# Attention over a cached K and V on one core: K transposed in 64-row tiles, P through the score banks, smaller loads

## The chip, the cores and the metric

One core of a Trainium2 chip. The metric is the device time of one execution in microseconds, lower is better; each time is the median of several executions. The kernel is one program with its own order of instructions for each of the five engines: TensorE (PE), VectorE (DVE), ScalarE (ACT), GpSimd (POOL) and SyncE (SP), which here issues the loads.

## The reference

Two independent blocks A and B, whose results are put side by side. For each of them:

```python
# x (16, 64, 640), k_cache and v_cache (16, 32, 512, 128), wq (640, 4096), wo (4096, 640), all bfloat16
q = (x @ wq).reshape(16, 64, 32, 128).transpose(0, 2, 1, 3)
scores = einsum("bhqd,bhkd->bhqk", q, k_cache) * 128 ** -0.5
p = softmax(scores, axis=-1)
o = einsum("bhqk,bhkd->bhqd", p, v_cache)
out = o.transpose(0, 2, 1, 3).reshape(16, 64, 4096) @ wo        # (16, 64, 640)
```

K and V of one batch and head are 512 x 128 values, 128 KB each. Over both blocks K and V are 268 MB, and every value is used once.

## The kernel before

**Tiling.** Two batches are worked on together, since 2 x 64 queries fill 128 partitions. A *step* g is one head of such a pair of batches, a *macro* m is two steps (two heads), a *chunk* c is four heads, a *group* is 16 heads of one pair of batches (`SPB` = 16 steps, four chunks). One pass holds half of the 32 heads of one block, so there are 4 passes of 8 groups, 32 groups, 128 chunks, 256 macros and 512 steps.

**One macro, operation by operation** (the names are those of the code; the line is that of the profile):
- LDK (L664) and LDV (L660) load K and V of four heads of one batch, 512 KB each, from SP's queue. LDWQ (L630) and LDWO (L638) load the weights of four heads, 640 KB each; LDX (L644) loads x by a transposing DMA.
- KX (L457): eight TensorE transposes, 128 rows by 128 columns, of K of both heads and one batch (index `sub`) into the bank KTB; each row of the K tile holds eight keys, so that the transposed order of the keys is permuted. KE (L466): VectorE copies the bank to `ktp_ring`.
- QP2 (L475): the queries of two heads, ten matmuls, into the first half of the bank QOB; QE2 (L484): ScalarE copies and scales them into `qT_ring`.
- SM (L496): scores of one step, one matmul for each batch in a 64-column tile of the array, into one of four score banks SB. MX (L505): negated row maximum on VectorE. EX (L511): exponential and row sum on ScalarE, into `p_ring`. RC2 (L517): reciprocals on VectorE. NM (L525): GpSimd scales P and puts its keys into the order of V, into `pn_ring`.
- TR2 (L534): eight transposes of P into the bank PTB. TE2 (L541, VectorE) or TA2 (L546, ScalarE, on 82 of the 256 macros) copies them to `pT_ring`.
- PV2 (L558): sixteen matmuls with V as the stationary operand, into the second half of QOB. OE2 (L566): ScalarE copies the result to `oT_ring`.
- OP2 (L574): two matmuls, the first 512 columns of the output, summed over the group in the bank OUTB. OX (L584): the last 128 columns, sixteen matmuls once per group, in score bank 0. OVP and OXP (L592, L597) store the sum of a first half of the heads, OVF and OXF (L602, L607) add that of the second half, and ST (L613) stores it to DRAM from ScalarE's queue.

**K by DMA.** In 11 of the 32 groups (`TGROUPS`) K of the second batch is not loaded plain and transposed on TensorE, but loaded by one transposing DMA for all 16 heads (LDKT, L651) into `kd_sb`; KX and KE with `sub` 1 are left out there.

**Order.** The order on PE, ACT, DVE and POOL is written out by hand for one chunk (two macros): a table for each engine with the kind, the offset in macros and a due time in a period of 6.7 us. The loads on SP are sorted by when they are needed and by when their buffer is free in that plan. The program then derives which instruction must wait for which from the buffers that they read and write, and drops the waits that others imply. Nothing is moved at run time: each engine runs its list in order and waits where it must. `NKB` = 4 chunks of K and `NVB` = 5 of V fit in SBUF, and `NW` = 6 weight slots of four heads.

The PSUM banks: 0 OUTB, 1 QOB, 2 to 5 SB, 6 PTB, 7 KTB.

Of the kernel before, what the change touches and what calls it, by code (L numbers as in the profile page):

```python
# [14 lines left out]
class Cfg:  # L15
    G = 4
    HH = 16
    NKB = 4
    NW = 6
    TGROUPS = (4, 6, 11, 13, 15, 19, 21, 23, 27, 29, 31)  # L20
    TLEAD = 1.0
    NVB = 5
    XLEAD = 1.5
    NQ = 3
    NKT = 5
    NP = 4
    NPN = 4
    NT = 2
    NO = 9
    NR = 8  # L30
    NS = 4
    PERIOD = 6.7
    PE_T = (("SM", 0, 0, 0.0), ("SM", 0, 1, 0.21), ("SM", 1, 0, 0.43), ("SM", 1, 1, 0.64), ("KX", 2, 1, 0.98),
            ("PV2", -3, 0, 1.43), ("TR2", -2, 0, 1.9), ("OP2", -4, 0, 2.35), ("KX", 3, 1, 2.78), ("QP2", 3, 0, 3.23),
            ("OP2", -3, 0, 3.79), ("OX", -3, 0, 4.2), ("KX", 3, 0, 4.22), ("PV2", -2, 0, 4.67), ("TR2", -1, 0, 5.14),
            ("KX", 4, 0, 5.59), ("QP2", 4, 0, 6.04))
    ACT_T = (("EX", 0, 0, 1.13), ("OE2", -3, 0, 2.1), ("EX", 0, 1, 2.49), ("TA2", -2, 0, 3.15), ("QE2", 3, 0, 4.0),
             ("EX", 1, 0, 4.4), ("OXP", -3, 0, 5.2), ("OE2", -2, 0, 5.34), ("EX", 1, 1, 5.73), ("OVP", -3, 0, 6.4),
             ("QE2", 4, 0, 6.65), ("ST", -3, 0, 6.68))
    DVE_T = (("MX", 0, 0, 0.44), ("MX", 0, 1, 1.06), ("RC2", -1, 0, 1.66), ("KE", 2, 1, 1.68), ("MX", 1, 0, 2.3),  # L40
             ("TE2", -2, 0, 2.6), ("RC2", 0, 0, 3.3), ("KE", 3, 1, 3.43), ("MX", 1, 1, 4.1), ("KE", 3, 0, 4.87),
             ("OXF", -3, 0, 5.3), ("OVF", -3, 0, 5.5), ("TE2", -1, 0, 5.79), ("KE", 4, 0, 6.4))
    POOL_T = (("NM", -1, 0, 1.95), ("NM", -1, 1, 2.8), ("NM", 0, 0, 4.2), ("NM", 0, 1, 5.05))
    TAIL_SPLIT = 2
    SLOT_NS = 3400.0
    DMA_NS = dict(LDK=3100.0, LDKT=9600.0, LDV=3100.0, LDWQ=3900.0, LDWO=4300.0, LDX=700.0)


class Op:
# [3 lines left out]
    def __init__(self, eng, kind, idx, reads=(), writes=(), dur=0.0, ts=None, aux=None):  # L53
        self.eng = eng
        self.kind = kind
        self.idx = idx
        self.reads = tuple(reads)
        self.writes = tuple(writes)
        self.sem = None
        self.count = None  # L60
        self.deps = []
        self.waits = []
        self.dur = dur
        self.ts = ts
        self.aux = aux
        self.dma = kind in ("LDK", "LDKT", "LDV", "LDX", "LDWQ", "LDWO", "ST")


def build_plan(dims, cfg):
# [3 lines left out]
    assert H % HH == 0 and HH % G == 0 and G % 2 == 0 and cfg.NR % 2 == 0 and B % 2 == 0  # L73
# [11 lines left out]
    MPP = NBP * MPG  # L85
    MPC = G // 2
# [11 lines left out]
    def by_dma(m, j=1):  # L98
        return j == 1 and m // MPG in cfg.TGROUPS

    tstart = [m for m in range(0, NMAC, MPG) if by_dma(m)]

# [3 lines left out]
    def kslot(m, j):  # L106
        return (4 * (m // 2) + (j if m % 2 == 0 else 3 - j)) % cfg.NKT

    def on_act(m):
        return m % 2 == 0 and not by_dma(min(m + 4, NMAC - 1))  # L110

    def make_op(kind, m, sub, ts):
        g0, g1 = 2 * m, 2 * m + 1
        if kind in ("KX", "KE") and by_dma(m, sub):
            return None
        ps_, bp, grp, h0 = step_info(g0)
        c = g0 // G
        if kind == "KX":
            return mk("pe", "KX", (m, sub), [("kn", c % cfg.NKB, g0 % G), ("kn", c % cfg.NKB, g1 % G), ("ident",)],
                      [("KTB",)], ts)  # L120
        if kind == "KE":
            return mk("dve", "KE", (m, sub), [], [("KTB",), ("ktp", kslot(m, sub))], ts)
        if kind in ("MX", "EX", "NM"):
            g = 2 * m + sub
            r = g % cfg.NR
            if kind == "MX":
                return mk("dve", "MX", g, [], [("SB", g % cfg.NS), ("negmax", r)], ts)
            if kind == "EX":
                return mk("act", "EX", g, [("negmax", r)], [("SB", g % cfg.NS), ("p", g % cfg.NP), ("rowsum", r)], ts)
            return mk("pool", "NM", g, [("p", g % cfg.NP), ("recip", r)], [("pn", g % cfg.NPN)], ts)  # L130
        r0, r1 = g0 % cfg.NR, g1 % cfg.NR
        if kind == "QP2":
            return mk("pe", "QP2", m, [("xT", bp), ("wq", wslot(ps_, h0 // G))], [("QOB",)], ts)
        if kind == "QE2":
            return mk("act", "QE2", m, [], [("QOB",), ("qT", m % cfg.NQ)], ts)
        if kind == "SM":
            kt = [("ktp", kslot(m, 0)), ("kd",) if by_dma(m) else ("ktp", kslot(m, 1))]
            return mk("pe", "SM", (m, sub), [("qT", m % cfg.NQ)] + kt, [("SB", (2 * m + sub) % cfg.NS)], ts)
        if kind == "RC2":
            return mk("dve", "RC2", m, [("rowsum", r0), ("rowsum", r1)], [("recip", r0), ("recip", r1)], ts)  # L140
        if kind == "TR2":
            return mk("pe", "TR2", m, [("pn", g0 % cfg.NPN), ("pn", g1 % cfg.NPN), ("ident",)], [("PTB",)], ts)
        if kind in ("TE2", "TA2"):
            if (kind == "TA2") != on_act(m):
                return None
            return mk("dve" if kind == "TE2" else "act", kind, m, [], [("PTB",), ("pT", m % cfg.NT)], ts)
        if kind == "PV2":
            return mk("pe", "PV2", m, [("pT", m % cfg.NT), ("v", c % cfg.NVB, g0 % G), ("v", c % cfg.NVB, g1 % G)],
                      [("QOB",)], ts)
        if kind == "OE2":  # L150
            return mk("act", "OE2", m, [], [("QOB",), ("oT", m % cfg.NO)], ts)
        if kind == "OP2":
            return mk("pe", "OP2", m, [("oT", m % cfg.NO), ("wo", wslot(ps_, h0 // G))], [("OUTB",)], ts)
        lo = grp * MPG
        last = h0 + 2 == SPB
        if kind == "OX":
            hi = m + 1
            if grp == NGRP - 1 and h0 + 6 == SPB:
                pass
            elif not last:  # L160
                return None
            elif grp == NGRP - 1:
                lo = m - 1
            return mk("pe", "OX", m, [("oT", i % cfg.NO) for i in range(lo, hi)]
                      + [("wo", wslot(ps_, i)) for i in sorted({(2 * i % SPB) // G for i in range(lo, hi)})],
                      [("SB", 0)], ts, aux=(lo, hi))
        if not last:
            return None
        if kind in ("OVP", "OXP") and ps_ % NHALF == 0:
            return mk("act", kind, m, [], [("OUTB",) if kind == "OVP" else ("SB", 0), ("outp", bp, kind[1])], ts,  # L170
                      aux=grp)
        if kind in ("OVF", "OXF") and ps_ % NHALF == 1:
            return mk("dve", kind, m, [("outp", bp, kind[1])],
                      [("OUTB",) if kind == "OVF" else ("SB", 0), ("out_sb", kind[1])], ts, aux=grp)
        if kind == "ST" and ps_ % NHALF == 1:
            return mk("act", "ST", m, [("out_sb", "V"), ("out_sb", "X")], [("out_dram", grp)], ts, aux=grp)
        return None

    templates = {"pe": cfg.PE_T, "dve": cfg.DVE_T, "pool": cfg.POOL_T, "act": cfg.ACT_T}
    at = {}  # L180
    for eng, tmpl in templates.items():
        offs = [t[1] for t in tmpl]
        for k in range(-(max(offs) + 1) // 2 - 1, (NMAC - min(offs)) // 2 + 1):
            for kind, off, sub, t in tmpl:
                m = 2 * k + off
                if 0 <= m < NMAC:
                    op = make_op(kind, m, sub, 2 * k + 2 * t / cfg.PERIOD)
                    if op is not None:
                        progs[eng].append(op)
                        at[kind, m, sub] = op.ts  # L190
# [10 lines left out]
    for ps_ in range(NPASS):  # L201
        for j in range(HG):
            m0 = ps_ * MPP + j * MPC
            i = ps_ * HG + j
            rq = ro = NEG
            if i >= cfg.NW:
                end = ((i - cfg.NW) // HG + 1) * MPP
                rq = at["QP2", end - MPG + ((i - cfg.NW) % HG) * MPC + MPC - 1, 0]
                ro = at["OX", end - 1, 0]
            add(rq, at["QP2", m0, 0], at["QP2", m0, 0], 0, "LDWQ", (ps_, j), [("wq", wslot(ps_, j))], (ps_, j),  # L210
                cfg.DMA_NS["LDWQ"] * G / 8.0)
            add(ro, at["OP2", m0, 0], at["OP2", m0, 0], 3, "LDWO", (ps_, j), [("wo", wslot(ps_, j))], (ps_, j),
                cfg.DMA_NS["LDWO"] * G / 8.0)

    def tload(m):
        return at["SM", m, 0] - cfg.TLEAD

# [540 lines left out]
```

## Time and profile before

| | us |
|---|---|
| median of 3 runs | 898.71 (897.31 to 901.26) |
| the profiled execution | 900.23 |
| its span, first to last instruction | 898.5 |
| PE busy | 857.5 |
| DVE, ACT, POOL busy | 746.6, 628.0, 413.8 |

The profile comes from one execution. Busy times sum the durations of an engine's instructions; since matmuls are pipelined and their ends are modelled, what a matmul costs is read from the distance of two starts. PEld is the loading of the stationary operand, which overlaps with PE. The granted TensorE clock was 0.996 of full speed in this execution. The loads move 292.06 MB on SP's queue.

### The profile page before, as it was taken

What the parts mean: (1) busy time and instruction counts of PE and PEld (TensorE: products, weight loads), DVE (VectorE), ACT (ScalarE), POOL (GpSimd) and SP (SyncE); (2) the same over time, 40 slices, a digit from 0 to 9 for tenths busy, and PEclk for the clock granted to TensorE, in tenths of its full rate; (3) what the DMA queues carried; (4) which work ended last, traced back from release to release, by engine and by line L of the source; (5) the groups of instructions that cost most, each with busy time, mean ns of one, the idle gap of its engine ahead of it and who ended that gap; (6) DMA issues with size and microseconds to landing.
All of it is one profiled execution on the core that took longest, in us unless ns stands there. A gap on an engine that the chain in (4) does not pass through costs nothing.

```text
span 898.5 us, 33204 instructions
## 1 busy us (share of the span) xinstructions
PE 857.5 (95%) x14016; PEld 691.1 (77%) x14144; DVE 746.6 (83%) x1398; ACT 628.0 (70%) x1651; POOL 413.8 (46%) x518
## 2 busy tenths in 40 slices
PE   4999989999999999999998998999999999999997
PEld 3777777878888877878786787778778777787875
DVE  2888878888888888888887887888888798888896
ACT  1776766777777777767676776777777676776774
POOL 0544444445444454544444444445454444545453
PEclk9999999999999999999999999999999999999999
DMA  9999999999999999999999999999999999999992
GB/s 304 336 340 365 318 272 365 295 361 365 363 366 368 286 361 322 319 369 270 364 361 368 367 260 365 309 324 366 294 363 363 367 370 284 367 286 365 315 333 77
DMA packets 315172, 296.81 MB, mean 330 GB/s; under 512 B 109200, under 2 KB 260752, under 8 KB 315024
## 3 DMA queue, kind: packets, MB, share of 16 engines
q1 hardware_dynamic: 312720, 292.06, 106.3%
q10 hardware_dynamic: 2304, 2.62, 0.9%
q8 instruction: 111, 1.82, 0.9%
q14 instruction: 37, 0.30, 0.1%
HBM read 266.34 MB, written 2.62 MB: 299 GB/s over the span
## 4 chain that ended last, share of the span: by engine, by line
PE 78%; DMA 9%; SPq 7%; DVE 3%; issue 1%; ACT 1%; DVEq 0%; ACTq 0%
PE ps L457 20%; PE ps L475 14%; PE ps L496 12%; PE ps L558 11%; PE ps L534 10%; PE ps L574 9%; DMA kn_ring<-in_B_k_cache_dram 5%; DMA kn_ring<-in_A_k_cache_dram 4%; SPq L651 3%; PE ps L584 3%; SPq L644 2%; DVE ktp_ring L466 1%; SPq L664 1%; DMA wq_sb<-in_A_wq_dram 1%; DVE negmax L505 1%
## 5 line engine op out<-in xcount | busy, mean ns | idle before, releaser
L525 POOL TENSOR_SCALAR pn_ring<-p_ring,recip 128x512 bf16<-128x512 bf16 x512 | 413.1, 843 | 476.1 <-DVE recip L517 475.7
L511 ACT ACTIVATE p_ring<-ps,negmax 128x512 bf16<-128x512 f32 x512 | 350.1, 684 | 100.0 <-DVE negmax L505 100.0
L466 DVE COPY ktp_ring<-ps 128x1024 bf16<-128x1024 bf16 x424 | 290.0, 684 | 82.1 <-PE ps L457 67.2
L505 DVE TENSOR_REDUCE negmax<-ps 128x1 f32<-128x512 f32 x512 | 337.3, 680 | 15.2 <-PE ps L496 4.9
L457 PEld LDWEIGHTS ps<-ident,kn_ring 128*128 128x128 bf16 x3392 | 205.3, 98 | 108.5 <-issue 46.5
L457 PE MATMUL ps<-ident,kn_ring 128*128 128x128 bf16 x3392 | 263.6, 221 | 21.1 <-DMA kn_ring<-in_A_k_cache_dram 11.8
L475 PE MATMUL ps<-xT_sb,wq_sb 128*128 128x128 bf16 x2560 | 187.8, 221 | 1.3 <-DMA wq_sb<-in_A_wq_dram 0.6
L558 PE MATMUL ps<-pT_ring,v_ring 128*128 128x64 bf16 x4096 | 162.0, 193 | 8.6 <-DMA v_ring<-in_B_v_cache_dram 3.1
L475 PEld LDWEIGHTS ps<-xT_sb,wq_sb 128*128 128x128 bf16 x2560 | 154.4, 99 | 16.9 <-ACT oT_ring L566 15.8
L558 PEld LDWEIGHTS ps<-pT_ring,v_ring 128*128 128x128 bf16 x4096 | 141.9, 98 | 28.5 <-issue 26.5
L484 ACT ACTIVATE qT_ring<-ps 128x256 bf16<-128x256 f32 x256 | 98.3, 384 | 86.1 <-PE ps L475 86.0
L534 PE MATMUL ps<-ident,pn_ring 128*128 128x128 bf16 x2048 | 156.4, 219 | 0.0
L566 ACT ACTIVATE oT_ring<-ps 128x256 bf16<-128x256 f32 x256 | 97.6, 381 | 75.3 <-PE ps L558 68.1
L541 DVE COPY pT_ring<-ps 128x1024 bf16<-128x1024 bf16 x174 | 119.5, 687 | 35.5 <-PE ps L534 35.5
L496 PE MATMUL ps<-ktp_ring,qT_ring 128*64 128x512 bf16 x848 | 137.3, 391 | 0.0
L574 PE MATMUL ps<-wo_sb,oT_ring 128*128 128x512 bf16 x384 | 124.5, 379 | 6.8
L534 PEld LDWEIGHTS ps<-ident,pn_ring 128*128 128x128 bf16 x2048 | 118.5, 98 | 0.0
L511 ACT ACTIVATION_READ_ACCUMULATOR p_ring<-ps,negmax 128x1 f32 x512 | 103.1, 201 | 0.0
L546 ACT ACTIVATE pT_ring<-ps 128x1024 bf16<-128x1024 bf16 x82 | 84.0, 1024 | 0.0
L496 PEld LDWEIGHTS ps<-ktp_ring,qT_ring 128*64 128x64 bf16 x848 | 47.1, 110 | 41.0 <-issue 2.1
L517 DVE RECIPROCAL recip<-rowsum 128x2 f32<-128x2 f32 x256 | 40.9, 160 | 14.7 <-ACT p_ring L511 14.6
L496 PE MATMUL ps<-kd_sb,qT_ring 128*64 128x512 bf16 x176 | 47.0, 390 | 0.0
(15 smaller groups left out, 152.0 us busy)
## 6 DMA issues: line engine op xcount, KB each, us to landing
v_ring<-in_A_v_cache_dram SPq DMA_DIRECT2D x128, 512.0 KB, 9.9
v_ring<-in_B_v_cache_dram SPq DMA_DIRECT2D x126, 512.0 KB, 9.8
kn_ring<-in_A_k_cache_dram SPq DMA_DIRECT2D x108, 512.0 KB, 9.4
kn_ring<-in_B_k_cache_dram SPq DMA_DIRECT2D x103, 512.0 KB, 9.3
wq_sb<-in_A_wq_dram SPq DMA_DIRECT2D x8, 640.0 KB, 9.9
wo_sb<-in_A_wo_dram SPq DMA_DIRECT2D x8, 640.0 KB, 10.7
wq_sb<-in_B_wq_dram SPq DMA_DIRECT2D x8, 640.0 KB, 9.7
wo_sb<-in_B_wo_dram SPq DMA_DIRECT2D x8, 640.0 KB, 10.3
```

The costliest lines, as they stand in the source:

```text
L457: ins = e.transpose(kt_ps[:, t8, :], kn_ring[:, c % NKB, j, hp, t8, :], ident[:, :])
L466: ins = e.tensor_copy(dst, src)
L475: ins = e.matmul(q_ps[:, sub * 128:(sub + 1) * 128], wq_sb[:, wslot(ps_, hh // G), kt, (hh % G) * DH:(hh % G + 1) * DH], xT_sb[:, kt, bp * ...
L484: ins = e.activation(qT_ring[:, m % NQ].rearrange("p s q -> p (s q)"), q_ps, ACTF.Copy, scale=scale)
L496: ins = e.matmul(s_bank(2 * m + sub)[64 * j:64 * j + 64, :], qT_ring[:, m % NQ, sub, 64 * j:64 * j + 64], kt, start=True, stop=True, tile_ ...
L505: ins = e.reduce_max(negmax[:, r:r + 1], s_bank(g), axis=AX.X, negate=True)
L511: ins = e.activation(p_ring[:, g % NP, :], s_bank(g), ACTF.Exp, bias=negmax[:, r:r + 1], scale=1.0, accum_out=rowsum[:, r:r + 1])
L525: ins = e.tensor_scalar(dst, src, recip[:, r:r + 1], 1.0, ALU.mult, ALU.mult)
L534: ins = e.transpose(pt_ps[:, sub, t, :], pn_ring[:, g % NPN, t * 128:(t + 1) * 128], ident[:, :])
L541: ins = e.tensor_copy(pT_ring[:, m % NT].rearrange("p s t q -> p (s t q)"), pt_ps_flat)
L558: ins = e.matmul(o_ps[:, col:col + 64], v_ring[:, c % NVB, j, gi, t, :], pT_ring[:, m % NT, sub, t, 64 * j:64 * j + 64], start=(t == 0), s ...
L574: ins = e.matmul(out_ps, oT_ring[:, m % NO, sub, :], wo_sb[:, wslot(ps_, hh // G), hh % G, 0:N0], start=(hh == 0), stop=(hh == SPB - 1))
```

## The change

- K: KX takes both batches of a macro at once. `kn_ring` becomes ten units of one macro; each unit has two tiles (one per batch) with the rows of head 0 in partitions 0 to 63 and of head 1 in 64 to 127. A transpose takes 64 rows (one head) instead of 128; the two heads alternate between the upper and the lower half of the array's rows (`tile_position`) and write to two banks (6 and 7). 32 transposes of 64 rows replace 2 x 8 of 128. KE copies both banks with one copy of 2048 elements per partition.
- P: TR writes a full tile (both steps of a macro) into score bank 0 or 1, in turn, instead of a bank of its own. TE copies it, on VectorE for even macros and on ScalarE for odd ones. `pT_ring` has four slots, not two.
- QP4, QE4, PV4, OE4 work on four heads at once where QP2, QE2, PV2, OE2 worked on two, and share the whole bank QOB. OX moves to score bank 2, always sixteen matmuls.
- No LDKT: all of K is transposed on TensorE, and `kd_sb` is gone.
- Loads: LDK and LDV are 256 KB each (two heads of one batch), LDWQ and LDWO are cut in two. Each load on SP waits until the fifth load before it has landed (`NDMA` = 5).
- The order written out for each engine is new, for a period of 6.15 us.

The core of the diff:

```diff
-    NKB = 4
+    NKU = 10
-    TGROUPS = (4, 6, 11, 13, 15, 19, 21, 23, 27, 29, 31)
-    NQ = 3
-    NKT = 5
+    NQ = 4
+    NKT = 3
-    NT = 2
-    NO = 9
+    NT = 4
+    NO = 10
-    PERIOD = 6.7
...
+    PERIOD = 6.15
+    PE_T = (("SM", 0, 0, 0.0), ("SM", 0, 1, 0.21), ("SM", 1, 0, 0.43), ("SM", 1, 1, 0.64), ("KX", 2, 0, 0.96),
+            ("PV4", -2, 0, 1.53), ("OP", -5, 0, 2.47), ("TR", -2, 0, 2.9), ("KX", 3, 0, 3.45), ("TR", -1, 0, 4.03),
+            ("OP", -4, 0, 4.47), ("OX", -5, 0, 4.9), ("QP4", 2, 0, 4.92))
+    ACT_T = (("EX", 0, 0, 1.13), ("EX", 0, 1, 1.79), ("OVP", -5, 0, 2.92), ("OE4", -2, 0, 2.95), ("EX", 1, 0, 3.52), ("EX", 1, 1, 4.18),
+             ("TE", -1, 0, 4.84), ("OXP", -5, 0, 5.9), ("ST", -5, 0, 6.0), ("QE4", 2, 0, 6.27))
+    DVE_T = (("MX", 0, 0, 0.44), ("MX", 0, 1, 1.06), ("KE", 2, 0, 1.68), ("RC2", 0, 0, 2.83), ("OVF", -5, 0, 2.92),
+             ("MX", 1, 0, 2.97), ("MX", 1, 1, 3.59), ("TE", -2, 0, 4.21), ("KE", 3, 0, 4.83),
+             ("OXF", -5, 0, 5.9), ("RC2", 1, 0, 5.98))
+    NDMA = 5
...
+    for op, old in zip(progs["sp"][cfg.NDMA:], progs["sp"]):
+        op.deps.append(old)
...
-        OUT_BANK, QO_BANK, PT_BANK, KT_BANK = 0, 1, 6, 7
+        OUT_BANK, QO_BANK, S_BANK0, KT_BANK = 0, 1, 2, 6
+        kt_ps = [ps[:, KT_BANK + r, :].bitcast(BF16) for r in range(2)]
+        kt_ps_both = ps[:, KT_BANK:KT_BANK + 2, :].bitcast(BF16)
+        ox_ps = ps[:, S_BANK0 + 2, 0:N1]
+        def pt_bank(m):
+            return ps[:, S_BANK0 + m % 2, :].bitcast(BF16)
...
         def em_KX(e, op):
-            for t8 in range(8):
-                ins = e.transpose(kt_ps[:, t8, :], kn_ring[:, c % NKB, j, hp, t8, :], ident[:, :])
+            for j in range(2):
+                for t in range(8):
+                    for r in range(2):
+                        half = slice(64 * r, 64 * r + 64)
+                        ins = e.transpose(kt_ps[r][:, 64 * (8 * j + t):64 * (8 * j + t) + 64],
+                                          kn_ring[half, op.idx % NKU, j, t, :], ident[half, half],
+                                          tile_position=(64 * r, 0))
...
         def em_KE(e, op):
+            ins = e.tensor_copy(ktp_ring[:, op.idx % NKT].rearrange("d r j s -> d r (j s)"), kt_ps_both)
...
+        def em_TR(e, op):
+                    ins = e.transpose(pt_bank(m)[:, 128 * i:128 * i + 128],
+                                      pn_ring[:, (2 * m + sub) % NPN, t * 128:(t + 1) * 128], ident[:, :])
...
+        def em_LDK(e, op):
+            src = blocks[blk][1][2 * bp + j, h0:h0 + 2].rearrange("hs (p t) d -> (hs p) (t d)", t=8)
+            ins = e.dma_start(kn_ring[:, m % NKU, j].rearrange("p t d -> p (t d)"), src)
...
+        def em_LDV(e, op):
+            src = blocks[blk][2][2 * bp + j, h0:h0 + 2].rearrange("g (p t) d -> p g (t d)", p=128)
+            ins = e.dma_start(v_ring[:, c % NVB, j, n:n + 2].rearrange("p g t d -> p g (t d)"), src)
```

## The prediction

> **What bounds the kernel now.** I read the page first, then the time line of TensorE over one steady period, then the windows view for the load side, then the waits.
>
> ```profile
> span 898.5 us, 33204 instructions
> PE 857.5 (95%) x14016; PEld 691.1 (77%) x14144; DVE 746.6 (83%) x1398; ACT 628.0 (70%) x1651; POOL 413.8 (46%) x518
> ...
> GB/s 304 336 340 365 318 272 365 295 361 365 363 366 368 286 361 322 319 369 270 364 361 368 367 260 365 309 324 366 294 363 363 367 370 284 367 286 365 315 333 77
> ```
>
> TensorE is busy 95% of the span, so its work per chunk is the first price. The second line to see is GB/s: it stands at 360 to 370 except in slices that hold a DMA transpose of K. One normal chunk on TensorE, from one score group (L496) to the next:
>
> ```profile
> 227.99 1.05 PE L496 MATMUL ps<-ktp_ring,qT_ring 128*64 128x512 bf16 x8
> 228.98 0.62 PE L457 MATMUL ps<-ident,kn_ring 128*128 128x128 bf16 x8
> 229.43 0.63 PE L558 MATMUL ps<-pT_ring,v_ring 128*128 128x64 bf16 x16
> 229.90 0.61 PE L534 MATMUL ps<-ident,pn_ring 128*128 128x128 bf16 x8
> 230.56 0.38 PE L574 MATMUL ps<-wo_sb,oT_ring 128*128 128x512 bf16 x1
> 230.78 0.61 PE L457 MATMUL ps<-ident,kn_ring 128*128 128x128 bf16 x8
> 231.23 0.72 PE L475 MATMUL ps<-xT_sb,wq_sb 128*128 128x128 bf16 x10
> ...
> 234.72 1.05 PE L496 MATMUL ps<-ktp_ring,qT_ring 128*64 128x512 bf16 x8
> ```
>
> Start to start is what counts, not the duration: 8 transposes of K take 0.45 us (56 ns each), 16 PV matmuls of 64 columns 0.47 (29.3 ns each), 10 query matmuls 0.65 into the scores but 0.55 elsewhere. The period is 6.73 us; where batch 1 of K comes by DMA it is 5.85 (two transposes of 8 fewer), and the output rest (L584) adds 0.89 once in four chunks. TensorE has no holes in it.
>
> ```profile
> core 0: us, PE busy (x) PEld busy (x) DVE busy (x) ACT busy (x) POOL busy (x), PEclk, DMA share, GB/s
> 200.00:290.00 90.00, 89.31 (x1491) 73.36 (x1503) 78.19 (x145) 68.53 (x176) 42.18 (x52) 1.00 1.08 366
> 162.00:178.00 16.00, 15.89 (x272) 13.06 (x271) 13.60 (x26) 11.84 (x31) 6.70 (x9) 1.00 1.21 277
> ...
> SPq L664 <- PE ps L457: 75.0, 79, 3.5
> ```
>
> In 90 undisturbed us PE is busy 89.3 us and the DMA engines are full at 366 GB/s; with a K transpose in flight they are fuller still and move 277. SP waits for a K slot only 75 us in all. So there are two bounds close together: TensorE, and loads. All loads are 292.06 MB (queue q1), which is 798 us at 366.
>
> **TensorE after, per chunk.** A chunk becomes: scores 4 x 0.216 + 0.025 (the first pair's extra) = 0.889; PV 32 x 0.0293 = 0.938; out projection 4 x 0.216 = 0.864; P transposes 16 x 0.056 = 0.896; query 20 x 0.056 = 1.12. These are unchanged in number, only grouped by four heads. K transposes: 2 x 32 instructions of 64 rows and 64 columns, alternating between two row halves. No row shows a row tile. The nearest rows are two: PV gives 29.3 ns for one instruction of 64 columns with its own weights, and the scores (L496), which use two column halves, show that two halves run side by side: 8 matmuls of 512 columns take 0.99 us, where one at a time would be 8 x 0.216 = 1.73; in the trace the second of a pair starts 4 ns after the first. So a pair costs 29.3 ns if the halves overlap and 58.6 if not. I take the first, because the pair of L496 is the nearer row: same engine, tiles, alternating halves. A group is then 16 x 0.0293 + 0.025 = 0.494, two per chunk 0.988, against 4 x 0.45 = 1.79 now.
>
> Changing the tile shape costs too: from the query to the scores the gap is 0.149 instead of 0.056, and from the last score to the next group 0.311 instead of 0.216, so 0.094 for each change. Now there are 2 per chunk. After it are 5 (query to scores, scores to K, K to PV, P to K, K to P): 0.47. The sum is 6.17. The same sum for the two periods of now gives 6.69 and 5.79 against 6.73 and 5.85, so I add 0.05: **6.22 us** per chunk. Bounds of a change: 0 to 0.15 (the whole gap). Bound of the added waits (each K group waits for two loads, each PV for four): the gap before a K group with two waits after P is 0.092 rather than 0.056, that before a PV with two waits is 0.056, so 0 to 0.036 each for about 8, up to 0.29 per chunk or 37 us; I take none, since most stand at a tile change, which drains anyway.
>
> **The other engines.** VectorE start to start is 0.60 for a row maximum, 0.60 for a copy of 1024, 0.07 to 0.24 for a reciprocal. After: 4 maxima, 1 copy of P, 2 reciprocals and 2 copies of 2048. No row shows 2048; between 0.60 (as 1024) and 1.20 (twice), I take 1.13 (0.60 plus the 0.53 that 1024 elements stream). Sum 2.4 + 0.6 + 0.4 + 2.3 = 5.7, at worst 5.9: hidden by TensorE's 6.22, with little left. The group's last additions (0.59 and 0.20) fall where TensorE has 0.89 more. ScalarE: 4 x 0.66 + 0.94 + two copies of 512 at most 2 x 0.56 = 4.7. GpSimd 4 x 0.81 = 3.2. P transposes into banks 0 and 1 wait for this chunk's exponentials of those banks, and the next scores wait for the copies out; by the order written, the first exponential ends some 1.8 us after the scores start and the first P group starts at 2.9 (0.89 + 0.09 + 0.49 + 0.09 + 0.94 + 0.43), and the copies out end before the next scores by 0.5 to 1.4. Both waits are covered; what covers them is that slack.
>
> **Loads.** Bytes stay; the transposes by DMA go (11, each 17.9 us to landing, with the engines at 268 to 304 GB/s around them). New is the cap: load n waits until load n-5 landed, everything behind it on SP waits too, and TensorE waits for that. Five loads hold 1.31 MB, 3.58 us at 366. What a load needs empty: 1.2 us from issue to the first packet (first K load), 0.5 from the last packet to the landing (last V load), 0.72 of data, 2.4 in all, below 3.58. The lone 160 KB store landed in 1.8. SP issues a load in 0.34 to 0.56 us when nothing backs up; 8.5 per chunk are 4.3. So the cap should not starve the engines: rate 366; the lowest undisturbed rows are 349 and 350 (V alone, below), and a starved queue would give less (rival 2). TensorE asks for 2.28 MB per 6.44 us on average, 354 GB/s. The price is that both bounds nearly meet.
>
> At this place a rule speaks against the change. The Trainium skill, "DMA: Bandwidth & Descriptors", section "Rules for kernel authors", asks for at least 1 MiB per DMA. The trace does not bear that out under a queue: the last four V loads are 256 KB and 872 to 876 and 875 to 880 us moved 349 and 350 GB/s, V alone, as 512 KB loads of V did.
>
> **Sum.** First scores at about 14 us (18.9 now; less is loaded ahead of them: 2.5 MB, at 366 that is 6.9 after the first packet at 3.4, then a query group and the scores); 127 periods x 6.22 = 790; 31 x 0.89 = 28; from the last scores to the end 15 (14.9 now; the chain through exponential, transposes, PV, output and store stays). Together 847, plus 4 for loads at the pass boundaries, where now some 20 us go. Span 851, with 1.7 around it 853; the median of the runs lies 1.5 below the profiled execution now (898.71 against 900.23), so **851**. The load bound alone gives 3 + 798 + about 6 after the last V = 807. Half a per cent, 4.5 us, is about what the runs can tell from no change.
>
> **Rivals.**
> 1. Row halves do not overlap (slower). Then 32 slots of 29.3 ns: 0.47 more per group, 256 groups, 120 us: **971**. For it: no row shows a row tile, every transpose loads 128 columns of weights, and PV never goes below 28 ns. Against: L496. It decides from (898.7 - 851) / 256 = 0.19 us more per group, 41 ns per pair. 0.13. The Trainium skill, "TensorE: Matmul & The Clock Gate", section "Wait — 56ns, not 53.3ns?", says that starts never come closer than about 25 ns however few the columns; by that rule a group is 0.80 and the time about 851 + 0.33 x 256 = 935. The trace disagrees for column halves (4 ns), and shows nothing for row halves.
> 2. The five-load cap starves the engines. At rate r the time is 292/r + 9: 866 at 341, 898 at 328. Any rate under about 347 sets the end. Each 0.05 us of gap per load costs 1094 x 0.05 = 55 us, less the 44 by which the load bound lies below. Between 866 and 894: 0.10; slower than 903: 0.07.
> 3. A chain of waits sets the period, not TensorE: the score banks now serve P too, and VectorE has half a us left. 0.2 to 0.3 more per chunk is 876 to 890. 0.10.
> 4. The edits cancel (the gain of the transposes is paid as tile changes of 0.15 and waits): 894 to 903, 0.04.
>
> **How the numbers follow.** My case, 838 to 866, has 0.52; below 838 (fewer drains, K to PV free) 0.04. Faster is 0.52 + 0.04 + 0.10 + 0.10 = 0.76, same 0.04, slower 0.13 + 0.07 = 0.20. The range runs from 836 to 900: above it lie the 0.20 of the slower cases, so 0.8 is inside.
>
> **What would show it.** Right: score groups 6.2 us apart, K groups (32 instructions) 0.5 to 0.6 from first start to the next group's, pairs a few ns apart; GB/s flat at 350 to 366. Rival 1: K groups of 0.8 to 1.0. Rival 2: PE idle before L457 or L558 on DMA, SP's queue waiting for landings, GB/s flat below 345. Rival 3: TensorE waiting for VectorE or ScalarE before scores or P. The forecast is wrong if the span lies outside 836 to 900, and its reason is wrong if K groups take over 0.7 or the period over 6.5.

## The result, and the profile after

The changed kernel takes **1020.74 us** (median of 4 runs, 1018.52 to 1029.17) against 899.99 us (897.31 to 901.37) for the kernel before on the same chip: a ratio of 1.136, 95% interval 1.132 to 1.140. The forecast was 851, with a range of 836 to 900. The profiled execution took 1020.85 us, its span was 1019.1. Here and below, ratios and intervals compare executions in the faster of two states of the chip, while medians are over all executions.

The page of the changed kernel, parts 1 to 4 and 6:

```profile
span 1019.1 us, 44106 instructions
PE 856.1 (84%) x18944; PEld 656.4 (64%) x18944; DVE 730.7 (72%) x1184; ACT 651.1 (64%) x1441; POOL 416.3 (41%) x518
...
GB/s 261 307 305 284 284 296 305 273 287 299 282 308 305 290 297 299 302 295 288 271 306 313 317 295 285 292 299 295 278 286 288 309 290 290 309 296 301 297 315 179
...
q1 hardware_dynamic: 242880, 292.10, 89.5%
...
DMA 89%; SPq 4%; PE 4%; issue 1%; DVE 1%; ACT 0%; DVEq 0%; ACTq 0%
...
kn_ring<-in_A_k_cache_dram SPq DMA_DIRECT2D x256, 256.0 KB, 4.5
```

No engine is the bound: TensorE went from 95% to 84% busy. The load rate is flat at 261 to 317 GB/s up to the last slice, where before it stood at 360 to 370 in the slices without a transposing load of K. Part 4 names the cause: 89% of the chain that ended last is waiting for a transfer. (The granted TensorE clock was 0.975 in this execution and 0.996 before; with TensorE on 4% of that chain, it is not what costs the 121 us.) And a load of 256 KB takes 4.5 us from issue to landing. TensorE in two chunks, from its time line:

```profile
405.00 1.05 PE L441 MATMUL ps<-ktp_ring,qT_ring 128*64 128x512 bf16 x8
405.99 0.64 PE L409 MATMUL ps<-ident,kn_ring 64*128 64x64 bf16 x32
407.35 1.09 PE L500 MATMUL ps<-pT_ring,v_ring 128*128 128x64 bf16 x32 [0.72 <-DMA v_ring<-in_A_v_cache_dram]
...
413.31 1.05 PE L441 MATMUL ps<-ktp_ring,qT_ring 128*64 128x512 bf16 x8
414.30 0.64 PE L409 MATMUL ps<-ident,kn_ring 64*128 64x64 bf16 x32
414.87 1.11 PE L500 MATMUL ps<-pT_ring,v_ring 128*128 128x64 bf16 x32
415.81 0.60 PE L516 MATMUL ps<-wo_sb,oT_ring 128*128 128x512 bf16 x2
416.24 0.61 PE L479 MATMUL ps<-ident,pn_ring 128*128 128x128 bf16 x8
416.79 0.64 PE L409 MATMUL ps<-ident,kn_ring 64*128 64x64 bf16 x32
417.36 0.62 PE L479 MATMUL ps<-ident,pn_ring 128*128 128x128 bf16 x8
417.81 0.59 PE L516 MATMUL ps<-wo_sb,oT_ring 128*128 128x512 bf16 x2
418.25 1.28 PE L425 MATMUL ps<-xT_sb,wq_sb 128*128 128x128 bf16 x20
419.46 0.84 PE L441 MATMUL ps<-ktp_ring,qT_ring 128*64 128x512 bf16 x6
```

The chunk from 413.31 to 419.46 is undisturbed, 6.15 us, and each K group (L409, 32 instructions) is 0.57 us from its start to the next group's. That is the TensorE that was forecast. The first chunk shows what became of it: PV (L500) stands 0.72 us for a V load. The waits of TensorE and of SP's queue, two views:

```profile
PE ps L500 <- DMA v_ring<-in_A_v_cache_dram: 61.8, 50, 2.5
PE ps L500 <- DMA v_ring<-in_B_v_cache_dram: 50.0, 43, 2.4
```

```profile
SPq L604 <- DMA kn_ring<-in_B_k_cache_dram: 67.1, 163, 2.5
SPq L595 <- DMA v_ring<-in_B_v_cache_dram: 58.3, 106, 2.6
SPq L604 <- DMA kn_ring<-in_A_k_cache_dram: 57.8, 157, 1.6
SPq L595 <- DMA v_ring<-in_A_v_cache_dram: 56.5, 108, 3.6
```

Each line is: who waited, for what, us in total, times, longest. SP stands before its K loads (L595) and V loads (L604) until an earlier load has landed, 240 us by these four rows alone; before, its longest row was 75 us for a free K slot. The queue is throttled by the cap, not by space. The middle of the run in the windows view (length, PE, PEld, DVE, ACT, POOL, then granted clock, DMA share, GB/s):

```profile
300.00:500.00 200.00, 172.09 (x3871) 132.26 (x3872) 150.26 (x246) 130.11 (x286) 84.44 (x104) 0.98 0.92 293
```

The semaphore records of this window show more of the 4.5 us. The end of a load is told by 16 signals, as many as there are DMA engines. The first comes 2.70 us after the issue, and the last, which is the landing, 1.6 us after the first (medians). The next load goes only when the last signal of the oldest one is there, so five loads move 5 x 0.262 MB / 4.5 us = 291 GB/s, against 293 measured.

### The profile page after: what moved, and what is told of

Same layout as the page of the kernel before. It is cut to its first block, busy times and chain, and to the rows that moved or that the text cites. A ratio compares the mean times of both kernels' runs of the same rounds, so it can differ in the third digit from the quotient of the medians.

```text
span 1019.1 us, 44106 instructions
## 1 busy us (share of the span) xinstructions
PE 856.1 (84%) x18944; PEld 656.4 (64%) x18944; DVE 730.7 (72%) x1184; ACT 651.1 (64%) x1441; POOL 416.3 (41%) x518
## 3 DMA queue, kind: packets, MB, share of 16 engines
q8 instruction: 151, 2.47, 1.0%
q10 hardware_dynamic: 2304, 2.62, 0.7%
HBM read 289.41 MB, written 2.62 MB: 287 GB/s over the span
## 4 chain that ended last, share of the span: by engine, by line
DMA 89%; SPq 4%; PE 4%; issue 1%; DVE 1%; ACT 0%; DVEq 0%; ACTq 0%
DMA v_ring<-in_A_v_cache_dram 24%; DMA kn_ring<-in_B_k_cache_dram 22%; DMA kn_ring<-in_A_k_cache_dram 21%; DMA v_ring<-in_B_v_cache_dram 20%; SPq L587 2%; SPq L595 2%; DMA wq_sb<-in_B_wq_dram 2%; PE ps L500 1%; DMA wq_sb<-in_A_wq_dram 1%; PE ps L516 1%; SPq L604 1%; PE ps L479 1%; PE ps L409 1%; DMA wo_sb<-in_A_wo_dram 0%; PE ps L425 0%
## 5 line engine op out<-in xcount | busy, mean ns | idle before, releaser
L417 DVE COPY ktp_ring<-ps 128x2048 bf16<-128x2048 bf16 x256 | 312.7, 1222 | 29.3 <-PE ps L409 28.9
L500 PE MATMUL ps<-pT_ring,v_ring 128*128 128x64 bf16 x4096 | 145.0, 195 | 114.8 <-DMA v_ring<-in_A_v_cache_dram 61.8
L500 PEld LDWEIGHTS ps<-pT_ring,v_ring 128*128 128x128 bf16 x4096 | 132.2, 99 | 127.1 <-issue 125.3
L409 PEld LDWEIGHTS ps<-ident,kn_ring 64*128 64x128 bf16 x8192 | 138.7, 96 | 92.1 <-issue 73.5
L409 PE MATMUL ps<-ident,kn_ring 64*128 64x64 bf16 x8192 | 168.4, 193 | 23.0 <-DMA kn_ring<-in_B_k_cache_dram 12.9
L425 PE MATMUL ps<-xT_sb,wq_sb 128*128 128x128 bf16 x2560 | 167.4, 222 | 14.5 <-DMA wq_sb<-in_A_wq_dram 12.3
L516 PE MATMUL ps<-wo_sb,oT_ring 128*128 128x512 bf16 x512 | 158.2, 392 | 5.2 <-DMA wo_sb<-in_A_wo_dram 3.6
L488 ACT ACTIVATE pT_ring<-ps 128x1024 bf16<-128x1024 bf16 x128 | 131.1, 1024 | 31.0 <-PE ps L479 28.2
L490 DVE COPY pT_ring<-ps 128x1024 bf16<-128x1024 bf16 x128 | 88.0, 688 | 80.9 <-PE ps L479 80.2
L508 ACT ACTIVATE oT_ring<-ps 128x512 bf16<-128x512 f32 x128 | 76.3, 596 | 106.8 <-PE ps L500 105.7
L434 ACT ACTIVATE qT_ring<-ps 128x512 bf16<-128x512 f32 x128 | 76.4, 597 | 89.4 <-PE ps L425 89.4
L516 PEld LDWEIGHTS ps<-wo_sb,oT_ring 128*128 128x128 bf16 x512 | 36.7, 100 | 6.9 <-DMA wo_sb<-in_A_wo_dram 4.2
```

What stands on the lines that cost most here:

```text
L409: ins = e.transpose(kt_ps[r][:, 64 * (8 * j + t):64 * (8 * j + t) + 64], kn_ring[half, op.idx % NKU, j, t, :], ident[half, half], tile_pos ...
L417: ins = e.tensor_copy(ktp_ring[:, op.idx % NKT].rearrange("d r j s -> d r (j s)"), kt_ps_both)
L425: ins = e.matmul(qo_ps[:, i * 128:(i + 1) * 128], wq_sb[:, wslot(ps_, hh // G), kt, i * DH:(i + 1) * DH], xT_sb[:, kt, bp * 128:(bp + 1) * ...
L488: ins = e.activation(dst, pt_bank(op.idx), ACTF.Copy)
L490: ins = e.tensor_copy(dst, pt_bank(op.idx))
L500: ins = e.matmul(qo_ps[:, col:col + 64], v_ring[:, c % NVB, j, i, t, :], pT_ring[:, (2 * c + i // 2) % NT, i % 2, t, 64 * j:64 * j + 64], ...
```

## The experiments

The first theory, **C**: the cap of five starves the DMA engines, whatever the size of a load. Its first rival, **S**: loads of 256 KB are slow however many are under way. The quoted expectations name theories by these letters and say what others hold where they bring them in. Times below are medians, with the ratio to the kernel before and its 95% interval. A *stop* is a place where two neighbouring matmuls of one group start more than 350 ns apart, after the first 30 us; its us are this distance of the starts.

**Without the cap, and with a cap of eight.**

```diff
-    NDMA = 5
+    NDMA = 100000
```

> The changed kernel without the cap: no load waits for the landing of another, only for its buffer. Theory C (the cap): five loads of 256 KB are too few, because a load takes 4.5 us from issue to landing in the changed kernel and not the 2.4 to 3.6 of the sum; without the cap the rate goes from 292 to 350 to 366 GB/s, TensorE no longer waits for loads, the score groups stand 6.15 us apart (as they do in the changed kernel wherever no load is late), and the time is 840 to 865 us. Theory S (the size): loads of 256 KB are slow by themselves; then the rate stays near 290 to 300 GB/s and the time within 2% of 1020. Theory M (the memory side: the changed kernel's own work slows the transfers): as S.

```diff
-    NDMA = 5
+    NDMA = 8
```

> The changed kernel with eight loads under way instead of five (2.1 MB instead of 1.3). Theory C: the rate rises with the bytes under way and nears the full 366 GB/s; landing takes 5.7 to 6.2 us, the time is 850 to 890. Theory S and M: within 2% of 1020, only the landing takes longer (about 7 us).

Without the cap: 947.53 us (1.053, 1.049 to 1.057). With eight: 900.37 us (1.003, 0.9998 to 1.006). So the cap is the larger part of the loss (taking it away gives back 73 us, raising it to eight 120, of 121 against the kernel before), and S falls, and with it M, by which the changed kernel's own work slows the transfers: loads of 256 KB move 360 GB/s and more once eight are under way. But both runs miss the range that C gave, neither comes near 851, and the uncapped one is slower than the one capped at eight, which C does not explain. The rate with the cap of eight, then rate and chain of the uncapped kernel:

```profile
GB/s 279 366 344 361 328 368 358 365 363 363 366 240 366 367 365 368 369 335 305 366 297 240 360 331 332 360 358 367 362 362 270 350 370 369 366 370 346 324 146 16
```

```profile
GB/s 289 363 343 368 326 366 319 326 319 347 332 139 368 369 369 320 316 326 314 364 269 224 368 304 356 367 287 332 353 363 159 341 369 369 318 337 329 327 162 15
...
PE 82%; issue 8%; SPq 4%; DVE 3%; ACT 1%; DMA 1%; POOL 0%; DVEq 0%; ACTq 0%
```

Waiting for transfers is down from 89% of the chain to 1%. New is 8% of "issue", time in which an engine waits for nothing that the profile shows. On TensorE's time line of the same kernel it looks like this:

```profile
143.32 0.55 PE L409 MATMUL ps<-ident,kn_ring 64*128 64x64 bf16 x25
145.81 0.29 PE L409 MATMUL ps<-ident,kn_ring 64*128 64x64 bf16 x7 [1.94 <-issue]
```

A group of 32 stops after its 25th instruction, where there is no wait in the program, for 2.1 us from start to start. There are 81 such stops, 87 us in all, and 65 of them (80 us) end 1.0 to 1.8 us, in the median 1.41 us, after a packet of 16 KB of the instruction queue (q8) has ended; 13% of the run's time lies at such a distance from a packet, so chance would give some 10. From this came theory **I**: with a deep load queue, TensorE's next instructions arrive late. Its first rival, **W**, holds that the rest of the loss is waiting among the engines. The page of the kernel after counts 151 packets of 16 KB, the page before 111; an instruction and its weight load are two, so a chunk has 296 instructions after and 221 before, and 256 of them, one packet (2.47 MB over 37,888 instructions are 65 bytes each), last 5.3 us at a period of 6.15 where they lasted 7.8 at 6.73.

**Loads of 512 KB with the cap of five.**

```diff
-                add(ready, first, first, 2, "LDK", (m, b), [("kn", m % cfg.NKU, b)], (m, b), cfg.DMA_NS["LDK"])
+            add(ready, first, first, 2, "LDK", (m, 0), [("kn", m % cfg.NKU, b) for b in range(2)], (m, 0), 2 * cfg.DMA_NS["LDK"])
...
-                add(ready, first, first, 2.5, "LDV", (c, i), [("v", c % cfg.NVB, i)], (c, i), cfg.DMA_NS["LDV"])
+                add(ready, first, first, 2.5, "LDV", (c, j), [("v", c % cfg.NVB, i) for i in (2 * j, 2 * j + 1)], (c, j), 2 * cfg.DMA_NS["LDV"])
...
```

> The changed kernel with K and V loads of 512 KB (both batches of a macro for K, four heads of a batch for V), still at most five under way. Theory C, bytes under way count: 2.6 MB, 350 to 366 GB/s, 840 to 870 us. Theory S: the loads are as large as before the change, so it is the same number; it differs from C only beside the run without the cap. Theory M: near 1020.

933.47 us (1.040, 1.034 to 1.045), far above the 840 to 870 that C gave. Five loads now hold 2.62 MB. Waits for loads are 6% of the chain, so the starving is gone, but there are 77 stops of 74 us. A cap in loads acts as a cap in bytes: in stops and time, five of 512 KB (2.4 MB under way in the median) lie between eight of 256 KB (2.1) and no cap (2.5).

**The cap alone, in the kernel before.** Three loads of 512 KB are 1.57 MB, a little more than the 1.31 of the change. Each load of K and V got a counter of its own for this.

```diff
...
+    for op, old in zip(progs["sp"][3:], progs["sp"]):
+        op.deps.append(old)
```

> The kernel before with one thing added: a load waits until the third load before it has landed, so that 1.5 MB are under way instead of 3.3 (6 to 7 loads). Each of its K and V loads gets its own semaphore for this. Theory C: the kernel before is slowed as well, to 300 to 325 GB/s between the DMA transposes, 980 to 1060 us. Theory S and M: it stays within 2% of 899, since sizes and work are the same.

1032.2 us (1.151, 1.144 to 1.158): as slow as the change, with nothing else of it. The windows view, of a stretch without transposing loads of K and of one with three of them:

```profile
200.00:290.00 90.00, 82.21 (x1316) 65.70 (x1317) 67.77 (x126) 59.58 (x156) 37.03 (x46) 0.96 0.94 307
300.00:500.00 200.00, 176.38 (x2801) 140.23 (x2799) 149.07 (x282) 120.81 (x321) 81.90 (x102) 0.95 0.99 292
```

Without a cap this kernel moved 366 GB/s in its stretch of 200 to 290 us and 335 in 300 to 500; with the cap it moves 307 and 292. Theory C holds from both sides, and S and M, by which this kernel should have stayed at 899, fall.

**Caps of seven and six.**

```diff
-    NDMA = 5
+    NDMA = 7
```

> The changed kernel with seven loads under way. The first four runs left two costs that go opposite ways: with five the loads are starved (292 GB/s, TensorE waits for K and V), without the cap TensorE stops in the middle of runs of equal matmuls, 81 times for 87 us in all, each time ending 1.3 to 1.5 us after a 16 KB packet of the instruction queue; with eight 43 times for 36 us. Theory I: many bytes of loads under way delay the fetch of TensorE's instructions. Then seven has fewer such stops (15 to 35 us) and loads at 340 to 350 GB/s when wanted, 885 to 930 us. Theory W (the rest with eight is waiting among engines, the cap does nothing to it): seven is slower than eight by the loads alone, 910 to 950, with as many stops as eight.

```diff
-    NDMA = 5
+    NDMA = 6
```

> The changed kernel with six loads under way (1.6 MB). Theory I and the cap: hardly any stops in mid-run (under 15 us), loads at 310 to 330 GB/s, 920 to 970 us. Theory W: the same time or above, but with some 36 us of stops in mid-run, as with eight.

Seven: 891.85 us (0.990, 0.986 to 0.993), the first version faster than the kernel before, by 1%. Six: 938.55 (1.042, 1.037 to 1.047). Bytes under way over the landing time give the rate: 6 x 0.262 / 4.85 = 324 GB/s (323 measured in 300 to 500 us), 7 x 0.262 / 5.2 = 353 (344 measured). From five to seven, one more under way lengthens a load by only 0.35 us. Bytes are not the whole of it: six loads of 256 KB moved 323 GB/s, the three of 512 KB in the kernel before, as many bytes, 307. The chain with seven:

```profile
DMA 58%; PE 34%; SPq 4%; issue 2%; DVE 1%; ACT 1%; DVEq 0%; ACTq 0%
```

Both losses are smaller here, but both are there: waiting for loads, and 19 stops of 13 us (15 to 35 us of them were expected). With six the stops are 7 of 4 us, where W asked for some 36 us.

**Is it the row halves that stop?** K by full tiles of 128 rows, 16 transposes per macro instead of 32, without a cap. Everything else of the change stays, but that the copy KE now puts the keys in order.

```diff
-    NDMA = 5
+    NDMA = 100000
...
-                    for r in range(2):
...
+                    ins = e.transpose(kt_ps[j][:, 128 * t:128 * t + 128], kn_ring[:, op.idx % NKU, j, t, :], ident[:, :])
...
```

> The changed kernel without the cap, and with K transposed in full 128-row tiles again: 16 transposes per macro instead of 32, so TensorE has 29,700 instructions with the weight loads instead of 37,900, and its period is longer, 6.15 + 2 x (0.896 - 0.494) - 3 x 0.094 = 6.67 us. Theory I: the stops in mid-run all but vanish, as in the kernel before (8 of them, 4 us), although as many loads are under way as in the run without the cap; the score groups are 6.6 to 6.7 us apart, 885 to 910 us, faster than the 947 without the cap in spite of the longer period. Theory W: the stops stay (60 us or more), 960 to 1000 us.

917.7 us (1.021, 1.019 to 1.023), a little above the range expected, with a period of 6.68 us and 3 stops instead of 81. Its loads are as deep in the queue as those of the uncapped change (2.9 MB under way in the median against 2.5, landing 7.9 to 8.2 us), so depth alone makes no stops. Its TensorE is hardly ever idle:

```profile
PE 889.1 (97%) x14720; PEld 735.5 (80%) x14848; DVE 727.8 (79%) x1184; ACT 650.8 (71%) x1441; POOL 417.8 (46%) x518
```

That leaves two readings: fewer instructions, or no row halves. The next run tells them apart.

**More instructions in the kernel before**, and no row halves: its query matmuls in two halves of 64 columns, its score matmuls in two of 256. The work is the same, the matmuls are 17,728 instead of 14,144.

```diff
+                for half in range(2):
+                    for kt in range(KT):
...
+                        ins = e.matmul(q_ps[:, c0:c0 + 64],
...
+            for half in range(2):
+                for j in range(2):
...
+                                   qT_ring[:, m % NQ, sub, 64 * j:64 * j + 64], kt,
...
```

> The kernel before, with more TensorE instructions for the same work: each query matmul in two halves of 64 columns and each score matmul in two halves of 256 columns (35,500 instructions with the weight loads instead of 28,300; the changed kernel has 37,900). By start-to-start times this alone costs 2 x 0.03 + 0.05 us per chunk, some 15 us. Theory I: stops in mid-run appear (30 us or more in all, where there were 4), 930 to 980 us. Theory W: no stops, 905 to 920 us.

928.89 us (1.034, 1.031 to 1.038), slightly under the range that theory I gave, and 53 stops of 40 us where the kernel before has 8 of 4 us; 51 of the 53 end 1.0 to 1.8 us after an instruction packet (chance would give 7). One of them, in a group of query matmuls:

```profile
205.40 0.57 PE L478 MATMUL ps<-xT_sb,wq_sb 128*128 128x64 bf16 x14
206.23 0.35 PE L478 MATMUL ps<-xT_sb,wq_sb 128*128 128x64 bf16 x6 [0.26 <-issue]
```

So the stops need no row halves, no small loads and nothing else of the change: more TensorE instructions over a deep load queue suffice. W falls, and theory I holds as far as the conditions go. That the instructions arrive late is read from where the stops end. A packet takes 1.1 us (median) in the kernel before and in the uncapped change alike, so it is not slower; whether it starts late, and why, the trace does not show.

**A version with slack on both sides.** The middle K group (odd macros) stands between the two groups of P, which use the full tile. Done in 128 rows it needs 16 instructions instead of 32 and saves two tile changes.

```diff
+                    if op.idx % 2:
+                        ins = e.transpose(kt_ps[j][:, 128 * t:128 * t + 128], kn_ring[:, op.idx % NKU, j, t, :], ident[:, :])
...
+                        continue
...
```

The copy KE of the odd macros puts the keys in the same order. Three caps: seven, eight, none.

> Cap of seven, and every second K group (the one that stands between the two groups of P, which have the same full tile) in 16 transposes of 128 rows instead of 32 of 64. TensorE has 280 instructions per chunk instead of 296 and two tile changes fewer, so its period is 6.15 + 0.40 - 0.19 = 6.36 us by the rows, and with the output rests 127 x 6.36 + 28 + 15 + 15 = 866 us if nothing waits. With seven loads under way the loads themselves gave 344 GB/s, 292/0.344 + 9 = 858 us at best. Cap theory (C) with instruction theory (I): both bounds are now below the 890 of the cap of seven alone, fewer stops, 868 to 885 us, period 6.36. If the cap of seven is what sets that kernel's 892 (its chain is 58% DMA) and the TensorE's period counts for nothing: 888 to 895, no difference from the cap of seven.

> The same with a cap of eight. If instruction fetch behind a deep queue (I) is what took the cap of eight from 866 to 900 us (43 stops, 36 us), then a TensorE that asks for 5% fewer instructions and 3% fewer bytes per us should find the queue less deep: 10 to 30 stops, 870 to 890 us. If the stops come with eight loads under way whatever the TensorE asks for, 895 to 910 us.

> The half-and-half transposes without a cap, so that the queue holds whatever the slots allow. With the cap of eight this kernel had 2 stops and 882 us; the change without a cap had 81 stops and 948 us at a period of 6.15. Theory I holds that a stop needs both a deep queue and a TensorE that runs through its instructions fast. 16 KB of instructions now last 5.8 us (5.3 in the change without a cap, 7.4 with full rows everywhere, where 3 stops came). Between these two: 15 to 40 stops, 15 to 45 us of them, 890 to 920 us. If the number of instructions had been the whole cause and depth none, the 2 stops stay: 878 to 886. If depth were the whole cause, 80 stops and 945 to 955.

One number in these texts is wrong: by the counted 16,896 matmuls a chunk has 264 instructions, not 280 (11% fewer, not 5%), and 16 KB last 6.2 us, not 5.8. Measured: seven 889.37 us (0.986, 0.982 to 0.991), eight **881.63** (0.979, 0.976 to 0.982), none 911.37 (1.013, 1.011 to 1.016). The cap of eight is the fastest kernel here, 2% under the kernel before. Its page, and some groups of one of its chunks:

```profile
PE 845.7 (96%) x16768; PEld 686.7 (78%) x16896; DVE 719.8 (82%) x1184; ACT 650.0 (74%) x1441; POOL 416.2 (47%) x518
...
PE 87%; DMA 6%; DVE 3%; issue 1%; ACT 1%; SPq 1%; DVEq 0%; ACTq 0%
```

```profile
418.09 1.05 PE L451 MATMUL ps<-ktp_ring,qT_ring 128*64 128x512 bf16 x8
419.08 0.64 PE L414 MATMUL ps<-ident,kn_ring 64*128 64x64 bf16 x32
...
421.47 1.06 PE L408 MATMUL ps<-ident,kn_ring 128*128 128x128 bf16 x16
422.36 0.61 PE L489 MATMUL ps<-ident,pn_ring 128*128 128x128 bf16 x8
...
424.45 1.05 PE L451 MATMUL ps<-ktp_ring,qT_ring 128*64 128x512 bf16 x8
```

The period is 6.36 us, as worked out from the rows, 0.21 longer than the change's, and yet the kernel is faster than every version with 6.15. At the same cap its span is 22 us shorter: the period costs 127 x 0.21 = 27 us more, 2 stops instead of 43 (10 to 30 were expected) give back 35, and the other 14 us, in part TensorE's shorter waits for ScalarE's exponentials (0.4 us instead of 7.3), stay open. With seven, the profiled execution, the fastest of six, had 2 stops as well, but 24% of its chain waits for loads, and five of the six lie between 881.73 and 891.80. The median misses the 868 to 885 of C with I and lies in the range of the other reading, by which the loads set the time at that cap; it can't be told from the 891.85 of seven alone. Without a cap 45 stops of 31 us came back, just above the 15 to 40 expected, so depth counts here too.

| kernel | under way, MB (median) | landing, us | 16 KB of TensorE's instructions last, us | stops: number, us |
|---|---|---|---|---|
| before | 3.3 | 9.3 to 9.9 | 7.8 | 8, 4 |
| before, more instructions | 2.6 | 7.5 to 8.9 | 6.2 | 53, 40 |
| change, none | 2.5 | 7.3 to 7.6 | 5.3 | 81, 87 |
| change, cap 5 of 512 KB | 2.4 | 6.8 to 7.0 | 5.3 | 77, 74 |
| change, cap 8 | 2.1 | 5.6 to 5.8 | 5.3 | 43, 36 |
| change, cap 7 | 1.8 | 5.2 to 5.3 | 5.3 | 19, 13 |
| change, cap 6 | 1.6 | 4.8 to 4.9 | 5.3 | 7, 4 |
| change as made, cap 5 | 1.3 | 4.4 to 4.5 | 5.3 | 19, 8 |
| 128 rows, none | 2.9 | 7.9 to 8.2 | 7.4 | 3, 2 |
| half 128, none | 2.9 | 7.8 to 8.2 | 6.2 | 45, 31 |
| half 128, cap 8 | 2.1 | 5.7 to 5.8 | 6.2 | 2, 1 |
| half 128, cap 7 | 1.8 | 5.2 | 6.2 | 2, 1 |

Landing times are those of K and V loads; the column on 16 KB is 256 x period / instructions per chunk. Without a cap the three versions of the change have more stops the faster the instructions go, and at one rate the stops grow with the depth. (Of the 19 with the cap of five, and of the 8 in the kernel before, only one each ends 1.0 to 1.8 us after an instruction packet; the others are another kind, whose cause stays open.) No single ratio of the two times orders all rows: landing over 16 KB is 1.2 in the kernel before, with hardly a stop, and 1.1 with the cap of eight and its 43.

## Why the prediction was wrong, by its own steps

**The step that failed is "Loads".** It took the time of a load as 2.4 us, the sum of latencies seen on an empty queue (1.2 to the first packet, 0.72 of data, 0.5 to the landing), compared this with the 3.58 us that five loads need at 366 GB/s, and concluded that the cap does not starve the engines. A load takes 4.5 us. For an empty queue the sum was nearly right: in the uncapped run three loads were issued with nothing else under way, and landed after 2.5 to 2.9 us. What it left out is what the four others under way do to a load. The signals show a part of it: the first comes at 2.70 us and the last 1.6 us later, against 0.3 to 0.6 in those three, and the landing, which alone lets the next load go, waits for the last. No run shows by itself that this spread is the whole cause. The trace of before held two hints. Seven of its loads of 512 KB were issued with a single transposing load ahead of them, and landed in 4.7 to 4.9 us, where the sum's terms give 3.1 (1.2, 1.43 of data, 0.5). And its landings of 9 to 10 us stood over 3.3 MB under way; 1.31 MB had never been seen to carry the full rate.

**Rival 2 was the outcome**, by the mechanism and with the signs described: PE idle before L500 on DMA, SP's queue waiting for landings, a flat rate below 345. Its own formula, 292/r + 9, gives 1006 at the 293 GB/s of the window; the loads' rate over the whole run was a little lower (292.1 MB in 1019 us are 287). What failed is its price and weight: 0.07 for anything slower than 903, with prices shown only down to 328 GB/s, because 2.4 us stood in the sum.

**The rule against the change.** The Trainium skill, "DMA: Bandwidth & Descriptors", section "Rules for kernel authors", asks for 1 MiB or more per DMA. The prediction set it aside. The windows on which it leaned were weak: the loads of 512 KB landed up to 878.8 us and the four of 256 KB from 878.7 to 881.6, so what moved from 872 to 876 was the larger ones for the most part. But the runs bear the prediction out in this: 256 KB loads reach 360 to 371 GB/s in many slices with eight or more under way. What decides most here is bytes under way: in loads of 256 KB, 1.3 MB give 293 GB/s, 1.6 give 323, 1.8 give 344.

**TensorE per chunk held.** Forecast 6.22 us (6.17 by the sum), measured 6.15. A pair of row halves was priced at 29.3 ns; measured, the second instruction starts 3 ns after the first and the next pair 26 ns later (medians). Rival 1 (halves one after the other, 58.6 ns) is refuted. The Trainium skill, "TensorE: Matmul & The Clock Gate", section "Wait — 56ns, not 53.3ns?", says that two starts never come closer than about 25 ns. Within such a pair that does not hold (3 ns); between one pair and the next it does (26). (The rival's price by that rule has a slip: 0.80 against 0.494 is 0.31 more per group, not 0.33, and gives 929.) Each of the five tile changes cost 0.093 to 0.096 us in the undisturbed chunk, where 0.094 was taken.

**The other engines held.** KE's copy of 2048 elements has a mean duration of 1.22 us; the copy of 1024 had 0.69 at 0.60 from start to start, so the 1.13 taken as start to start fits. Rival 3, a period set by waits among the engines, does not show: undisturbed chunks are 6.15 us apart. Rival 4, gains and costs of the edits cancelling on TensorE, does not either.

**"Sum" was some 11 us low even without the cap's loss.** The uncapped change without its stops would be 949.4 - 87.3 = 862 us of span, that with a cap of eight 899.1 - 36.1 = 863, against 851. In the kernel with a cap of eight, first scores came at 15.1 us instead of 14, from the last scores to the end were 17.2 instead of 15, the output rest (L526) costs 0.91 in half of the groups and 1.39 in the others where 0.89 was taken (some 8 us), and the first seven chunks take 8 us more than seven periods and one rest; the period, 6.15 instead of 6.22, gives 9 us back.

**Left out altogether: the stops.** No term and no rival had them, and the trace of before hid them (8 of 4 us). They did not cost the change its time (19 of 8 us, one of them after an instruction packet). But they are why taking the cap away did not give 862: the remedy for one loss fed the other. The forecast's remark that "both bounds nearly meet" was the warning: TensorE at 6.15 us asks for 2.28 MB per chunk and its share of the output rest, some 358 GB/s of 366, which leaves little to make up a stop.

## What to carry to other kernels

Size a cap on loads in flight by bytes and by the landing time seen under load: rate = bytes under way / landing time, and raise it until the rate stops growing, no further. When a stage is cut to finer instructions, work out how long 16 KB of that engine's instructions last (stops were many here at 5.3 and 6.2 us over a deep queue, few at 7.4 and 7.8), and look for pauses inside a group with "issue" as their cause. Where two bounds meet, a slightly longer period can win, as 6.36 us over 6.15 did here by 10 us between the best of each.

## What was not expected of the hardware

A load's landing is the last of 16 signals, and with five loads under way it comes 1.6 us after the first in the median, 2.7 at the 95th percentile. In the kernel before it is 1.7 and 2.9. There, over 3.3 MB under way, 366 GB/s are reached all the same.

TensorE pauses in the middle of a group, for up to 3.0 us from start to start, where nothing in the program waits; in the kernels with many stops the pauses that end near an instruction packet end 1.41 to 1.44 us (medians) after the end of its 16 KB. The Trainium skill, "Runtime: NRT & Kernel Launch", section "Instruction fetch mechanics", says that instructions come in blocks of 16 KiB, 256 of them, over a DMA queue of the sequencer's own, mostly hidden. The runs agree on the size; how well it is hidden depends here on the load queue and on the rate of instructions, from 2 stops to 81. That the packets wait in the DMA engines behind the loads is the likeliest reading, and no run here shows it by itself.
